# Attention followed by two MLPs: inner values of the first MLP by 768-token blocks, and y's remainders partly on GpSimd

## The chip, the cores and the metric

The kernel runs on one core of a Trainium2 chip. The metric is the device time of the whole program in microseconds (us), median of three runs. Engines are called PE (TensorE, matrix products), ACT (ScalarE), DVE (VectorE), POOL (GpSimd) and SP (SyncE, which issues DMAs). PSUM is the accumulator memory that PE writes; SBUF is the working memory.

## What is computed

```python
a  = softmax(phi, over the 576 positions)          # 4 batches, 8 heads, 32 memory slots
km, vm = a.T @ k, a.T @ v                           # 32 x 64 per head
x  = softmax(q @ km.T / 8) @ vm                     # joined over heads: 2304 tokens x 512
y  = ((x @ w_a) * (x @ w_b)) @ w_out                # first MLP,  1536 inner values
h  = y @ w_in
out = where(h > 0, h, exp(min(h, 0)) - 1) @ w_out2  # second MLP, 2048 inner values
```

The weights arrive as 64-bit floats. Each product is made from two parts per operand: a rounded part ("hi") and the remainder ("lo"), and three products hi·hi, hi·lo, lo·hi are summed in PSUM.

## The kernel before

**Stages.** An attention prologue runs over the 4 batches of 576 tokens (to about 75 us of the span). Then the first MLP (MLP1) runs, to 421 us, and the second (MLP2), to the end. The 2304 tokens are therefore 4 batches `b` of S = 576 for MLP1, and 3 blocks `t` of TB = 768 for MLP2. The result `y` of MLP1 is kept in three SBUF tiles of one block each.

**MLP1.** The inner values come in NF1 = 12 groups `f` of 128. For each `f`, `step_u` (line 483) forms the weights of the group folded with vm (two steps `u(f,0)`, `u(f,1)`), which needs the two converted units `("ab", f, 0)` and `("ab", f, 1)`. `steps_ab(f, b)` (line 576) makes two PE steps of 12 products of 288 columns each: x·w_a, copied out by ACT (line 597), and x·w_b, multiplied into that by DVE (line 599). One step later ACT rounds the product into `gh` (line 600), and two steps later DVE takes the remainder into `gl` (line 601). `gh` and `gl` are tiles of one group and one batch, nine buffers each. `run_o1(b, f)` (line 650) then multiplies all groups of batch `b` that are waiting (up to G = 3) by w_out: `steps_o1` (line 621) makes four PE steps, one for each 128 of the 512 outputs, each of 6 products of 288 columns per waiting group. The result is added to `y` from PSUM: by ACT where it is the first sum of these tokens (line 640), otherwise by DVE (line 642). A batch crosses block borders, so `y_parts` (line 606) cuts this into one, two or three instructions.

**Order.** All engines run in the order in which the program issues (the schedule is written by hand). The list at lines 667 to 674 fixes the order of the `u` and `ab` steps. A call of `run_o1` is appended to `pend` when `(f + b) % 3 == 2` (line 689) and made two `ab` calls later (three for f = 0), line 687. `step` (line 229) issues the PE work of a step, then, in the order "0f1a2", a share of the weight conversion ("f"), the step's own evacuation ("a"), and what was deferred to this step ("2", the default place).

**Weight conversion.** Each 64-bit unit is converted by seven small DVE pieces, slots 0 to 6 of `piece` (line 147), with ACT helping. `fill(amount)` issues pieces by credit: 1 per `ab` and `u` step, 3 per o1 step, 2.5 per `h` step, 3 or 6 per o2 step. `weights(key)` (line 192) issues all pieces that are still missing for a unit at the place where PE needs it. Slot 3 also issues, on POOL's queue, the DMA that loads the unit three further on (lines 98 to 106, 170). Pieces are held back when four short or four long units are alive.

**Border of the two MLPs.** After the last `ab` step the loop at line 707 runs what is left of o1: one group of b = 1, two of b = 2 and three of b = 3. In between, `split_y` (line 699) cuts a block of `y` into `yh` (ACT) and `yl` (DVE), four chunks of 128 x 768 per block, at once where it is called. Block 2 is split at line 717.

**MLP2.** `step_h(f, t)` (line 721) makes 24 products of 384 columns with `yh`/`yl` of block t, then a chain of ACT and DVE work forms the activation. For f = 0 the blocks come in the order 0, 1, 2. `steps_o2` (line 759) makes the products with w_out2, 512 columns each. PSUM serves four tiles in turn, each of which holds one step's result until it has been evacuated.

Of the kernel before, what the change touches and what calls it, by code (L numbers as in the profile page):

```python
# [7 lines left out]
F32 = mybir.dt.float32  # L8
F32R = mybir.dt.float32r
# [4 lines left out]
AF = mybir.ActivationFunctionType  # L14
ALU = mybir.AluOpType
# [6 lines left out]
def attention_then_two_mlps(ctx, tc, q, kv, kv_left, phi, w_ab, w_o1, w_i2, w_o2, out):  # L22
# [13 lines left out]
    nc = tc.nc  # L36
    B, P, KC, S = q.shape
# [4 lines left out]
    NF1, NF2 = w_ab.shape[0], w_i2.shape[0]  # L42
# [1 line left out]
    SM = NJ * P  # L44
    LEFT = S - SM
    HS = S // 2
    G = 3
    TB = 768
    NB = NT // TB
    HB = TB // 2  # L50
# [14 lines left out]
    def pone(name):  # L65
        return pstile(name)[:, 0] if len(pss) == 2 else ps1.tile([P, 512], F32, tag="one", name=name)

    def split_sb(hi, lo, src):
        nc.scalar.activation(out=hi, in_=src, func=AF.Copy)  # L69
        nc.vector.tensor_tensor(out=lo, in0=src, in1=hi.bitcast(F32), op=ALU.subtract)  # L70


    NRAW, NSHORT, NLONG = 3, 4, 4
# [140 lines left out]
    RATE_AB, RATE_U, RATE_O1 = 1.0, 1.0, 3.0  # L214
    RATE_H, RATE_O2 = 2.5, 3.0
# [5 lines left out]
    def defer(steps, fn, at=2):  # L221

        later.append([steps, fn, at])
# [257 lines left out]
    u_t, g_t = {}, {}  # L481
# [28 lines left out]
    with tc.manual_schedule():  # L510
# [65 lines left out]
        def steps_ab(f, b, amount):  # L576
            u = u_t.pop((f, b))
            a_sb = pb.tile([P, 2, HS], F32, tag="a_sb", name="a_sb", bufs=3)
            flat = a_sb.rearrange("p a s -> p (a s)")
            gh = pb.tile([P, S], F32R, tag="gh", name="gh", bufs=9)  # L580
            gl = pb.tile([P, S], F32R, tag="gl", name="gl", bufs=9)
            g_t[f, b] = gh, gl
            for n in range(2):
                ps = pstile("ab_ps")

                def pe():
                    for kk in range(2):
                        for i, (w, x) in enumerate(((0, xhi), (0, xlo), (1, xhi))):
                            for h in range(2):
                                nc.tensor.matmul(  # L590
                                    ps[:, h, 0:HS], u[:, kk, w, n * P:n * P + P], x[b][:, kk, h * HS:(h + 1) * HS],
                                    start=(kk == 0 and i == 0), stop=(kk == 1 and i == 2),
                                )

                def evac():
                    if n == 0:
                        nc.scalar.activation(out=a_sb, in_=ps[:, :, 0:HS], func=AF.Copy)  # L597
                    else:
                        nc.vector.tensor_tensor(out=a_sb, in0=a_sb, in1=ps[:, :, 0:HS], op=ALU.mult)  # L599
                        defer(1, lambda: nc.scalar.activation(out=gh, in_=flat, func=AF.Copy))  # L600
                        defer(2, lambda: nc.vector.tensor_tensor(
                            out=gl, in0=flat, in1=gh.bitcast(F32), op=ALU.subtract))

                step(pe, evac, amount)

        def y_parts(c, t0, ps):


            if t0 // TB == (t0 + S - 1) // TB:
                o = t0 % TB  # L610
                yield ps[:, :, 0:HS], yv[t0 // TB][:, c, o:o + S].rearrange("p (h s) -> p h s", h=2)
                return
            for h in range(2):
                done = 0
                while done < HS:
                    blk, o = divmod(t0 + h * HS + done, TB)
                    w = min(HS - done, TB - o)
                    yield ps[:, h, done:done + w], yv[blk][:, c, o:o + w]
                    done += w

        def steps_o1(b, fs, amount):
            for c in range(KC):
                ps = pstile("o1_ps")

                def pe():
                    cc = slice(c * P, (c + 1) * P)
                    for n, f in enumerate(fs):
                        wh, wl = weights(("o1", f))
                        gh, gl = g_t[f, b]
                        for i, (w, g) in enumerate(((wh, gh), (wh, gl), (wl, gh))):  # L630
                            for h in range(2):
                                nc.tensor.matmul(  # L632
                                    ps[:, h, 0:HS], w[:, cc], g[:, h * HS:(h + 1) * HS],
                                    start=(n == 0 and i == 0), stop=(n == len(fs) - 1 and i == 2),
                                )

                def evac():
                    for src, dst in y_parts(c, b * S, ps):
                        if fs[0] == 0:
                            nc.scalar.activation(out=dst, in_=src, func=AF.Copy)  # L640
                        else:
                            nc.vector.tensor_tensor(out=dst, in0=src, in1=dst, op=ALU.add)

                step(pe, evac, amount)
            for f in fs:
                g_t.pop((f, b))

        used1 = {}

        def run_o1(b, f):  # L650
            fs = [x for x in range(NF1) if (x, b) in g_t and x <= f]
            steps_o1(b, fs, RATE_O1)
            for x in fs:
                used1[x] = used1.get(x, 0) + 1
                if used1[x] == B:
                    drop(("o1", x))

        last = B - 1
# [18 lines left out]
        for kind, *args in order:  # L677
            if kind == "do":
                args[0]()
            elif kind == "u":  # L680
                step_u(*args, RATE_U)
            else:
                f, b = args
                steps_ab(f, b, RATE_AB)
                for e in pend:
                    e[0] -= 1
                if pend and pend[0][0] <= 0:
                    run_o1(*pend.pop(0)[1:])
                if (f + b) % G == G - 1:
                    pend.append([2 if f else 3, b, f])  # L690
        es_u.close()
        es_a.close()

# [2 lines left out]
        pc = es_2.enter_context(tc.tile_pool(name="pc", bufs=2, reuse_waits="tile"))  # L696
        ysp = {}

        def split_y(blk, pool):
            hi = pool.tile([P, KC, TB], F32R, tag=f"yh{blk}", name=f"yh{blk}", bufs=1)  # L700
            lo = pool.tile([P, KC, TB], F32R, tag=f"yl{blk}", name=f"yl{blk}", bufs=1)
            for c in range(KC):
                split_sb(hi[:, c], lo[:, c], yv[blk][:, c])
            ysp[blk] = hi, lo

        flush_later()
        for b in range(B):
            if any((x, b) in g_t for x in range(NF1)):
                run_o1(b, NF1 - 1)
            if b == 1:  # L710
                split_y(0, pc)
            if b == 2:
                split_y(1, pc)
        es_b.close()
        es_0.close()
        pd = es_2.enter_context(tc.tile_pool(name="pd", bufs=2, side="right", reuse_waits="tile"))
# [4 lines left out]
        def step_h(f, t):  # L721
            ps = pstile("h_ps")
            yh, yl = ysp[t]
            wh, wl = [x.rearrange("p (c f) -> p c f", c=KC) for x in weights(("i2", f))]
            gh = pd.tile([P, TB], F32R, tag="g2h", name="g2h", bufs=6)
            gl = pd.tile([P, TB], F32R, tag="g2l", name="g2l", bufs=6)
            g2[f, t] = gh, gl

            def pe():
                for c in range(KC):  # L730
                    for i, (w, x) in enumerate(((wh, yh), (wh, yl), (wl, yh))):
                        for h in range(2):
                            nc.tensor.matmul(  # L733
                                ps[:, h, 0:HB], w[:, c], x[:, c, h * HB:(h + 1) * HB],
                                start=(c == 0 and i == 0), stop=(c == KC - 1 and i == 2),
                            )

            e = pc.tile([P, 2, HB], F32, tag="e", name="e", bufs=2)
            flat = e.rearrange("p a s -> p (a s)")
            th = pc.tile([P, 2, HB], F32, tag="th", name="th", bufs=1)  # L740


            def negative():
                nc.scalar.activation(out=e, in_=ps[:, :, 0:HB], func=AF.Relu, scale=-1.0)  # L744

            def functions():
                nc.scalar.activation(out=th, in_=e, func=AF.Tanh, scale=-0.5)
                nc.scalar.activation(out=e, in_=e, func=AF.Exp, scale=-1.0)  # L748

            def both_signs():  # L750
                nc.vector.scalar_tensor_tensor(out=e, in0=e, scalar=1.0, in1=th, op0=ALU.add, op1=ALU.mult)  # L751
                nc.vector.tensor_tensor(out=e, in0=e, in1=ps[:, :, 0:HB], op=ALU.max)
                defer(1, lambda: nc.scalar.activation(out=gh, in_=flat, func=AF.Copy), 0)
                defer(1, lambda: nc.vector.tensor_tensor(
                    out=gl, in0=flat, in1=gh.bitcast(F32), op=ALU.subtract), 1)

            step(pe, [negative, functions, both_signs], RATE_H, ORDER_H)

        def steps_o2(t, fs, last):

# [115 lines left out]
```

## Time and profile before

| | us |
|---|---|
| median of 3 runs (828.2 to 829.19) | 829.03 |
| the profiled execution's own time | 829.17 |
| its span, first to last instruction | 827.4 |
| PE busy | 790.7 |
| DVE busy | 593.1 |
| ACT busy | 396.5 |
| POOL busy | 40.5 |

The rows further down come from the profiled execution. In the groups of instructions the last column is the time for which the engine stood idle just ahead of these instructions, and what released it. In the chain of waits a row tells which work the end of the program hung on at that moment. Ends of matrix products are modelled, so rates are read from the spacing of long runs of them.

### The profile page before, as it was taken

What the parts mean: (1) busy time and instruction counts of PE and PEld (TensorE: products, weight loads), DVE (VectorE), ACT (ScalarE), POOL (GpSimd) and SP (SyncE); (2) the same over time, 40 slices, a digit from 0 to 9 for tenths busy, and PEclk for the clock granted to TensorE, in tenths of its full rate; (3) what the DMA queues carried; (4) which work ended last, traced back from release to release, by engine and by line L of the source; (5) the groups of instructions that cost most, each with busy time, mean ns of one, the idle gap of its engine ahead of it and who ended that gap; (6) DMA issues with size and microseconds to landing.
All of it is one profiled execution on the core that took longest, in us unless ns stands there. A gap on an engine that the chain in (4) does not pass through costs nothing.

```text
span 827.4 us, 14253 instructions
## 1 busy us (share of the span) xinstructions
PE 790.7 (96%) x6032; PEld 729.4 (88%) x6032; DVE 593.1 (72%) x979; ACT 396.5 (48%) x608; POOL 40.5 (5%) x87
## 2 busy tenths in 40 slices
PE   4588899999999999999999999999999999999997
PEld 3477789999999999999999899888999889998896
DVE  3488988678877886667778842787777786776464
ACT  2434576554434433343357754556654556553350
POOL 2000000000000000000000000000000000000000
PEclk9599999999999999999999999999999999999999
DMA  9882022112220221001000200111111110100006
GB/s 325 293 289 102 1 83 97 58 71 78 77 77 27 78 77 51 27 27 51 26 27 26 77 26 15 62 50 35 45 52 51 51 51 26 51 0 1 1 1 229
DMA packets 16815, 57.79 MB, mean 70 GB/s; under 512 B 1776, under 2 KB 1776, under 8 KB 16752
## 3 DMA queue, kind: packets, MB, share of 16 engines
q0 software_dynamic: 9360, 34.08, 11.7%
q1 hardware_dynamic: 7392, 22.81, 7.8%
q8 instruction: 47, 0.77, 0.4%
q14 instruction: 16, 0.13, 0.0%
HBM read 52.17 MB, written 4.72 MB: 69 GB/s over the span
## 4 chain that ended last, share of the span: by engine, by line
PE 91%; DVE 4%; ACT 2%; DMA 2%; issue 0%; SPq 0%; ACTq 0%; DVEq 0%
PE o_ps L776 24%; PE h_ps L733 24%; PE o_ps L632 18%; PE ab_ps L590 18%; PE u_ps L497 2%; PE sc L426 2%; DMA raw<-in_w_ab_dram 1%; PE pk L386 1%; DVE ssm L460 1%; DVE y L465 1%; PE tp_x L473 0%; PE tp_a L362 0%; DVE y L453 0%; DVE smx L452 0%; DMA phi_t<-in_phi_dram 0%
## 5 line engine op out<-in xcount | busy, mean ns | idle before, releaser
L590 PE MATMUL ab_ps<-xhi,u 128*128 128x288 f32 x768 | 139.4, 298 | 3.7 <-ACT xhi L69 2.9
L590 PEld LDWEIGHTS ab_ps<-xhi,u 128*128 128x128 f32 x768 | 114.1, 189 | 9.0 <-issue 3.2
L776 PE MATMUL o_ps<-ulh,g2h 128*128 128x512 f32 x288 | 113.7, 395 | 0.0
L776 PE MATMUL o_ps<-ull,g2h 128*128 128x512 f32 x288 | 113.6, 394 | 0.0
L776 PE MATMUL o_ps<-ulh,g2l 128*128 128x512 f32 x288 | 103.0, 395 | 0.0
L751 DVE SCALAR_TENSOR_TENSOR e<-e,th 128x768 f32<-128x768 f32 x48 | 46.0, 958 | 75.0 <-ACT e L748 74.6
L733 PE MATMUL h_ps<-yh,usl 128*128 128x384 f32 x384 | 97.8, 335 | 0.0
L733 PE MATMUL h_ps<-yl,ush 128*128 128x384 f32 x384 | 97.7, 335 | 0.0
L733 PE MATMUL h_ps<-yh,ush 128*128 128x384 f32 x384 | 97.7, 335 | 0.0
L744 ACT ACTIVATE e<-h_ps 128x768 f32<-128x768 f32 x48 | 39.0, 813 | 95.8 <-PE h_ps L733 93.6
L632 PE MATMUL o_ps<-gh,ulh 128*128 128x288 f32 x384 | 82.5, 296 | 0.6 <-DVE u L507 0.4
L632 PE MATMUL o_ps<-gl,ulh 128*128 128x288 f32 x384 | 82.2, 296 | 0.0
L632 PE MATMUL o_ps<-gh,ull 128*128 128x288 f32 x384 | 82.2, 296 | 0.0
L590 PE MATMUL ab_ps<-xlo,u 128*128 128x288 f32 x384 | 82.1, 295 | 0.0
L597 ACT ACTIVATE a_sb<-ab_ps 128x576 f32<-128x576 f32 x48 | 31.3, 652 | 86.4 <-PE ab_ps L590 86.4
L733 PEld LDWEIGHTS h_ps<-yh,ush 128*128 128x128 f32 x384 | 69.5, 188 | 1.3
L599 DVE TENSOR_TENSOR a_sb<-a_sb,ab_ps 128x576 f32<-128x576 f32 x48 | 36.1, 752 | 46.5 <-PE ab_ps L590 44.8
L733 PEld LDWEIGHTS h_ps<-yh,usl 128*128 128x128 f32 x384 | 69.4, 188 | 0.0
L733 PEld LDWEIGHTS h_ps<-yl,ush 128*128 128x128 f32 x384 | 69.3, 188 | 0.0
L776 PEld LDWEIGHTS o_ps<-ulh,g2l 128*128 128x128 f32 x288 | 54.0, 187 | 13.2
L776 PEld LDWEIGHTS o_ps<-ulh,g2h 128*128 128x128 f32 x288 | 54.0, 187 | 12.6
L776 PEld LDWEIGHTS o_ps<-ull,g2h 128*128 128x128 f32 x288 | 54.0, 187 | 12.5
(93 smaller groups left out, 1338.4 us busy)
## 6 DMA issues: line engine op xcount, KB each, us to landing
raw<-in_w_o_dram POOLq DMA_DIRECT2D x27, 512.0 KB, 3.5
raw<-in_w_ab_dram POOLq DMA_DIRECT2D x22, 512.0 KB, 3.6
kv_t<-in_kv_dram SPq DMA_DIRECT2D x16, 512.0 KB, 10.1
raw<-in_w_i_dram POOLq DMA_DIRECT2D x16, 512.0 KB, 3.6
y<-in_q_dram SPq DMA_DIRECT2D x8, 576.0 KB, 8.8
out_dram<-y SPq DMA_DIRECT2D x8, 512.0 KB, 2.9
phi_t<-in_phi_dram SPq DMA_DIRECT2D x3, 576.0 KB, 11.8
left_t<-in_kv_left_dram SPq DMA_DIRECT2D x4, 256.0 KB, 12.1
```

What stands on the lines that cost most here:

```text
L386: nc.tensor.matmul(pk[M * h:M * h + M, D * u:D * u + D], a[0:P if j < NJ else LEFT, u, j, M * h:M * h + M], rows, start=(j == 0), stop=(j ...
L426: nc.tensor.matmul(sc[:, u, j * P:(j + 1) * P], qs[u][:, t, j * P:(j + 1) * P], kt[:, u, t * P:(t + 1) * P], start=(t == 0), stop=(t == 1))
L460: nc.vector.tensor_reduce(out=sm, in_=at, op=ALU.add, axis=AX.X)
L497: nc.tensor.matmul(ps[j:j + M, o, k * 256:k * 256 + 256], vt[r, 2 * k + c, 2 * p + o], w[r, c * 256:c * 256 + 256], start=True, stop=True, ...
L590: nc.tensor.matmul(ps[:, h, 0:HS], u[:, kk, w, n * P:n * P + P], x[b][:, kk, h * HS:(h + 1) * HS], start=(kk == 0 and i == 0), stop=(kk == ...
L597: nc.scalar.activation(out=a_sb, in_=ps[:, :, 0:HS], func=AF.Copy)
L599: nc.vector.tensor_tensor(out=a_sb, in0=a_sb, in1=ps[:, :, 0:HS], op=ALU.mult)
L632: nc.tensor.matmul(ps[:, h, 0:HS], w[:, cc], g[:, h * HS:(h + 1) * HS], start=(n == 0 and i == 0), stop=(n == len(fs) - 1 and i == 2),)
L733: nc.tensor.matmul(ps[:, h, 0:HB], w[:, c], x[:, c, h * HB:(h + 1) * HB], start=(c == 0 and i == 0), stop=(c == KC - 1 and i == 2),)
L744: nc.scalar.activation(out=e, in_=ps[:, :, 0:HB], func=AF.Relu, scale=-1.0)
L751: nc.vector.scalar_tensor_tensor(out=e, in0=e, scalar=1.0, in1=th, op0=ALU.add, op1=ALU.mult)
L776: nc.tensor.matmul(ps[:, k, :], g[:, c * P:(c + 1) * P], w, start=(f == fs[0] and i == 0), stop=(f == fs[-1] and i == 2),)
```

## The change

- `gh` and `gl` become tiles of one group and one 768-token block, seven buffers each. A batch writes one or two parts: batch 0 lies in block 0; batch 1 puts 192 tokens in block 0 and 384 in block 1; batch 2 puts 384 in block 1 and 192 in block 2; batch 3 lies in block 2. ACT and DVE round and subtract part by part.
- o1 runs per block: six products of 384 columns per group and step; the sum with `y` is one instruction of 768 columns; `y_parts` is gone.
- `run_o1(t, f)` is appended when batch `b = t + 1` of a group with `(f + t) % 3 == 2` was issued, and made one `ab` call later (two for f = 0).
- At the border the o1 steps convert weights at 0.5 instead of 3.0 pieces a step, and the `h` steps of f = 0 at 0.5 instead of 2.5.
- The splits of blocks 0 and 1 are deferred, chunk c by c + 1 steps, and their `yl` goes to GpSimd; block 2 stays on DVE, at once.

```diff
-    G = 3
+    G, NG = 3, 7
-    def split_sb(hi, lo, src):
+    def split_sb(hi, lo, src, eng=nc.vector):
         nc.scalar.activation(out=hi, in_=src, func=AF.Copy)
-        nc.vector.tensor_tensor(out=lo, in0=src, in1=hi.bitcast(F32), op=ALU.subtract)
+        eng.tensor_tensor(out=lo, in0=src, in1=hi.bitcast(F32), op=ALU.subtract)
...
-            gh = pb.tile([P, S], F32R, tag="gh", name="gh", bufs=9)
-            gl = pb.tile([P, S], F32R, tag="gl", name="gl", bufs=9)
-            g_t[f, b] = gh, gl
+            parts, done = [], 0
+            while done < S:
+                t, o = divmod(b * S + done, TB)
+                if o == 0:
+                    g_t[f, t] = [pb.tile([P, TB], F32R, tag=x, name=x, bufs=NG) for x in ("gh", "gl")]
+                w = min(S - done, TB - o)
+                parts.append((flat[:, done:done + w], *[x[:, o:o + w] for x in g_t[f, t]]))
+                done += w
...
-                        defer(1, lambda: nc.scalar.activation(out=gh, in_=flat, func=AF.Copy))
-                        defer(2, lambda: nc.vector.tensor_tensor(
-                            out=gl, in0=flat, in1=gh.bitcast(F32), op=ALU.subtract))
+                        defer(1, lambda: [nc.scalar.activation(out=gh, in_=a, func=AF.Copy) for a, gh, _ in parts])
+                        defer(2, lambda: [nc.vector.tensor_tensor(out=gl, in0=a, in1=gh.bitcast(F32), op=ALU.subtract)
+                                          for a, gh, gl in parts])
...
-                                    ps[:, h, 0:HS], w[:, cc], g[:, h * HS:(h + 1) * HS],
+                                    ps[:, h, 0:HB], w[:, cc], g[:, h * HB:(h + 1) * HB],
...
-                    for src, dst in y_parts(c, b * S, ps):
-                        if fs[0] == 0:
-                            nc.scalar.activation(out=dst, in_=src, func=AF.Copy)
-                        else:
-                            nc.vector.tensor_tensor(out=dst, in0=src, in1=dst, op=ALU.add)
+                    src, dst = ps[:, :, 0:HB], yv[t][:, c].rearrange("p (h s) -> p h s", h=2)
+                    if fs[0] == 0:
+                        nc.scalar.activation(out=dst, in_=src, func=AF.Copy)
+                    else:
+                        nc.vector.tensor_tensor(out=dst, in0=src, in1=dst, op=ALU.add)
...
-                if (f + b) % G == G - 1:
-                    pend.append([2 if f else 3, b, f])
+                t = b - 1
+                if b and (f + t) % G == G - 1:
+                    pend.append([1 if f else 2, t, f])
...
-                split_sb(hi[:, c], lo[:, c], yv[blk][:, c])
+                (defer if blk + 1 < NB else now)(c + 1, lambda c=c: split_sb(hi[:, c], lo[:, c], yv[blk][:, c],
+                                                              nc.gpsimd if blk + 1 < NB else nc.vector))
...
-        for b in range(B):
-            if any((x, b) in g_t for x in range(NF1)):
-                run_o1(b, NF1 - 1)
-            if b == 1:
-                split_y(0, pc)
-            if b == 2:
-                split_y(1, pc)
+        for t in range(NB):
+            if any((x, t) in g_t for x in range(NF1)):
+                run_o1(t, NF1 - 1, 0.5)
+            if t + 1 < NB:
+                split_y(t, pc)
...
-            step(pe, [negative, functions, both_signs], RATE_H, ORDER_H)
+            step(pe, [negative, functions, both_signs], RATE_H if f else 0.5, ORDER_H)
```

## Rows read from the trace of the kernel before

**Rows 1.** The page: busy time by engine, and slices of the span.

```profile
PE 790.7 (96%) x6032; PEld 729.4 (88%) x6032; DVE 593.1 (72%) x979; ACT 396.5 (48%) x608; POOL 40.5 (5%) x87
PE   4588899999999999999999999999999999999997
...
PEclk9599999999999999999999999999999999999999
```

**Rows 2.** Chain of waits in order of time: start us, us, what.

```profile
141.72 9.60 PE o_ps L632 x72
...
411.42 9.82 PE o_ps L632 x72
421.24 25.01 PE h_ps L733 x144
...
463.00 12.60 PE o_ps L776 x54
475.60 12.50 PE h_ps L733 x72
```

**Rows 3.** PE's waits over the span: us in total, times, longest.

```profile
PE ab_ps L590 <- ACT xhi L69: 2.9, 1, 2.9
...
PE ab_ps L590 <- ACT y L640: 0.8, 1, 0.8
PE o_ps L632 <- DVE u L507: 0.4, 1, 0.4
```

**Rows 4.** Timeline around the first o1 steps: start us, us, instruction, idle before.

```profile
113.28 0.42 PE L632 MATMUL o_ps<-gh,ulh 128*128 128x288 f32 x2
...
113.55 0.75 DVE L599 TENSOR_TENSOR a_sb<-a_sb,ab_ps 128x576 f32<-128x576 f32 x1 [1.37 <-PE ab_ps L590]
...
114.22 0.75 DVE L601 TENSOR_TENSOR gl<-a_sb,gh 128x576 fp32r<-128x576 f32 x1
...
114.89 0.42 DVE L178 TENSOR_TENSOR lw<-lw,p 128x512 bf16<-128x512 bf16 x1
...
115.34 0.69 DVE L185 TENSOR_TENSOR ush<-a,lw 128x512 f32<-128x512 f32 x1
...
116.57 0.66 PE L497 MATMUL u_ps<-ush,vt 64*32 64x256 f32 x16
```

**Rows 5.** Groups by line: count, busy us, mean ns, idle before.

```profile
L754 DVE TENSOR_TENSOR g2l<-e,g2h 128x768 fp32r<-128x768 f32 x48 | 45.8, 954 | 9.6 <-ACT g2h L753 9.5
L642 DVE TENSOR_TENSOR y<-o_ps,y 128x288 f32<-128x288 f32 (+3 forms) x120 | 45.7, 429 | 19.2 <-PE o_ps L632 19.0
L753 ACT ACTIVATE g2h<-e 128x768 fp32r<-128x768 f32 x48 | 40.5, 844 | 35.4 <-DVE e L752 35.4
L601 DVE TENSOR_TENSOR gl<-a_sb,gh 128x576 fp32r<-128x576 f32 x48 | 36.1, 751 | 4.6 <-ACT gh L600 4.5
L600 ACT ACTIVATE gh<-a_sb 128x576 fp32r<-128x576 f32 x48 | 32.7, 680 | 10.0 <-DVE a_sb L599 9.8
```

**Rows 6.** Timeline of DVE just behind an o1 start at 388.49 us.

```profile
388.76 0.76 DVE L599 TENSOR_TENSOR a_sb<-a_sb,ab_ps 128x576 f32<-128x576 f32 x1 [0.72 <-PE ab_ps L590]
389.43 0.75 DVE L601 TENSOR_TENSOR gl<-a_sb,gh 128x576 fp32r<-128x576 f32 x1
390.10 0.42 DVE L160 TENSOR_SCALAR a<-a 128x512 f32<-128x512 f32 x1
```

**Rows 7.** Groups of POOL by form: count, busy us, mean ns.

```profile
L103 POOL DMA_DIRECT2D raw<-in_w_o_dram x27 | 14.5, 537 | 307.1 <-DVE p L173 131.4 <-ACT g2h L753 114.4 <-DVE a L168 20.0
L522 POOL COPY pair<-ident 128x32 f32<-128x32 f32 x8 | 1.4, 211 | 0.0
L520 POOL COPY y<-ident 128x64 f32<-128x64 f32 x4 | 0.9, 237 | 0.1
```

**Rows 8.** Timeline of DVE at the border of the two MLPs.

```profile
406.92 3.55 DVE L70 TENSOR_TENSOR yl<-y,yh 128x768 fp32r<-128x768 f32 x4
...
413.57 3.56 DVE L70 TENSOR_TENSOR yl<-y,yh 128x768 fp32r<-128x768 f32 x4
```

More of the change, by code (lines that the diff above doesn't have):

```diff
@@ L599, in evac, with steps_o1 @@
                         nc.vector.tensor_tensor(out=a_sb, in0=a_sb, in1=ps[:, :, 0:HS], op=ALU.mult)
-                        defer(1, lambda: nc.scalar.activation(out=gh, in_=flat, func=AF.Copy))
-                        defer(2, lambda: nc.vector.tensor_tensor(
-                            out=gl, in0=flat, in1=gh.bitcast(F32), op=ALU.subtract))
+                        defer(1, lambda: [nc.scalar.activation(out=gh, in_=a, func=AF.Copy) for a, gh, _ in parts])
+                        defer(2, lambda: [nc.vector.tensor_tensor(out=gl, in0=a, in1=gh.bitcast(F32), op=ALU.subtract)
+                                          for a, gh, gl in parts])
                 step(pe, evac, amount)
[L606 to L621, printed above, removed]
+        def steps_o1(t, fs, amount):
             for c in range(KC):
@@ L628, in pe @@
                         wh, wl = weights(("o1", f))
-                        gh, gl = g_t[f, b]
+                        gh, gl = g_t[f, t]
                         for i, (w, g) in enumerate(((wh, gh), (wh, gl), (wl, gh))):
@@ L637, in evac, with run_o1 @@
                 def evac():
-                    for src, dst in y_parts(c, b * S, ps):
-                        if fs[0] == 0:
-                            nc.scalar.activation(out=dst, in_=src, func=AF.Copy)
-                        else:
-                            nc.vector.tensor_tensor(out=dst, in0=src, in1=dst, op=ALU.add)
+                    src, dst = ps[:, :, 0:HB], yv[t][:, c].rearrange("p (h s) -> p h s", h=2)
[3 more added lines that the diff above has]
+                        nc.vector.tensor_tensor(out=dst, in0=src, in1=dst, op=ALU.add)
                 step(pe, evac, amount)
             for f in fs:
-                g_t.pop((f, b))
+                g_t.pop((f, t))
         used1 = {}
-        def run_o1(b, f):
-            fs = [x for x in range(NF1) if (x, b) in g_t and x <= f]
-            steps_o1(b, fs, RATE_O1)
+        def run_o1(t, f, amount=RATE_O1):
+            fs = [x for x in range(NF1) if (x, t) in g_t and x <= f]
+            steps_o1(t, fs, amount)
             for x in fs:
                 used1[x] = used1.get(x, 0) + 1
-                if used1[x] == B:
+                if used1[x] == NB:
                     drop(("o1", x))
@@ L697, in attention_then_two_mlps, with now @@
         ysp = {}
+        def now(_, fn):
+            fn()
         def split_y(blk, pool):
```

## Prediction, made before the changed kernel was run

> **What bounds the kernel now.** I read the page's busy times and slices first: PE is busy for 790.7 of 827.4 us, and from the sixth slice on every slice but the last has the digit 9 [rows 1]. DVE, the next, has 593.1. So whatever the change saves on DVE or ACT is worth nothing by itself; it must shorten PE's own work or a wait of PE. The chain of waits confirms it: between 130 us and the end it is made of PE pieces that follow each other without gaps, and the border of the MLPs, at 421 us, is one of those joints [rows 2]. The view of PE's waits leaves little to win behind the prologue: one wait of 0.8 us and one of 0.4 us, both near 121 to 123 us, and the 2.9 us on ACT at 93 us, where the attention of the last batches still runs beside MLP1 [rows 3].
>
> So the questions are: what does PE pay for the new shape of product, and does a new wait open?
>
> **The products (the gain).** Before, o1 has 12 groups x 4 batches x 4 steps x 6 = 1152 products of 288 columns. After, 12 x 3 x 4 x 6 = 864 of 384. The columns are the same 331,776. A run of 72 products of 288 takes 9.60 us, 133.3 ns each; 72 of 384 in the `h` steps, same operand types and 128x128 stationary tile, take 12.50 us, 173.6 ns, and 144 take 25.01 us, 173.7 ns [rows 2]. So 1152 x 0.1333 = 153.6 us becomes 864 x 0.1737 = 150.1 us: 3.5 us less, all on the path. Put otherwise: at 2.4 GHz, the level granted there [rows 1], the columns take 120 and 160 ns, so some 13.5 ns stick to every product whatever its width, and 288 products fewer save 288 x 0.0133 - 864 x 0.0004 = 3.5 us.
>
> The Trainium skill (TensorE: Matmul & The Clock Gate, "Back-to-back issue gap") gives a warm gap of columns divided by 2.4 GHz plus about 2.5 ns. By that 288 products fewer would save only 0.7 us; our two rows carry five times that overhead, so I go by the rows, and keep the rule as a rival.
>
> **A wait that the new order opens (a loss).** I followed the credit rule through the list of steps. Before, the first o1 call (batch 2, group 0) lies ahead of `u(2,0)`, and its four steps issue 12 pieces, two of which finish the unit ("ab", 2, 1) that `u(2,0)` needs. After, that call waits for batch 3 and falls behind `u(2,0)` and `u(2,1)`. At `u(2,0)` two pieces (slots 5 and 6) are missing, and `weights` issues them on the spot, behind DVE's product and remainder of the step before. The trace shows just this queue: product at 113.55, remainder at 114.22, slot 5 at 114.89, slot 6 from 115.34 to 116.03, while PE does its o1 products from 113.28 and comes to `u` at 116.57 [rows 4]. Without these, PE starts `u(2,0)` at 113.28, does its first half in about half a microsecond (an estimate: 16 instructions of the 0.66 us row, which overlaps its successor) and stands until 116.1: 2.3 us lost. Bounds: 0 (if the pieces run earlier) and 3.0 (one more DVE instruction of 0.75 us ahead of them).
>
> Against that, the two waits of 0.8 and 0.4 us came from the same burst of 12 pieces in 3.2 us of PE, with one ACT queue behind [rows 3]. Replayed with the new order, the bursts meet steps of 1.04 and 2.08 us instead of 0.8 and 1.6, and PSUM tiles come free 0.7 us ahead of PE or better. I take them as gone, with 1.2 us as the other end. Net at this place: 2.3 - 1.2 = 1.1 us lost (0 to 2.3).
>
> **More, smaller instructions.** Batches 1 and 2 round and subtract in two parts: 24 more on ACT, 24 more on DVE. From 576 and 768 columns, ACT goes 680 to 844 ns, so 0.19 us is fixed; DVE 751 to 954, so 0.14 us [rows 5]: 4.6 and 3.4 us, on engines with room. Only in the prologue is ACT on the path, once, ahead of the 2.9 us wait [rows 3]: 0.2 us. The sums with `y` become 44 DVE instructions of about 0.95 us, 42 us where there were 45.7 in 120 [rows 5]; off the path, nothing.
>
> **Less slack for o1.** A call now comes one `ab` call after its last batch, not two. Its last group's `gl` is then issued behind the newest product on DVE. At an o1 start of 388.49 us DVE takes that product at 388.76 and a remainder at 389.43, done at 390.18, 1.7 us after PE began [rows 6]. PE needs it only after two groups of 6 products and two more: 14 x 0.174 = 2.4 us. 0.7 us is left, so I charge nothing; if DVE is behind by one more instruction of 0.75 us, PE waits under 0.3 us in each of some 10 calls, 3 us in all. Weights: counted to the end, no other unit is missing when PE asks; the lead is 8 pieces or more in the later `u` steps and o1 calls (it was 13 or more), and from `h(1,1)` on the count is the same as before. At most 7 inner tiles are alive, as many as there are.
>
> **The border.** The left-over o1 shrinks from six groups of 576 tokens to three of 768; that moves products, it removes none. From the end T of the last `ab` step PE has 72 x 0.174 = 12.5 us of o1, then the `h` steps of 4.17 us each. POOL gets eight remainders of 128x768 and one DMA issue. No row shows its subtraction. A copy takes 211 ns for 32 columns and 237 for 64 [rows 7]: 185 ns and 0.81 ns a column, so 0.81 us for one input over 768; a second read pass gives 1.43, a write pass on top 2.06. I take 1.75 us, between the last two, as reads and writes may share a path. The first can start when ACT has made the last `gh` and the first `yh`: 0.3 + 0.75 + 0.68 + 0.85 = 2.6 us after T. End of the eighth: 2.6 + 0.54 + 8 x 1.75 = 17.1 us. The last chunk of block 1 is wanted at 12.5 + 4.17 + 3 x 1.04 + 0.35 = 20.1 us. It is hidden, with 3 us. At 2.06 us each it ends at 19.6, still hidden; if DVE's four remainders of 0.95 us for block 2 had to take turns with it there, 3.8 us later, and PE would wait 3.3. DVE is freed of 2 x 3.55 us [rows 8], but it wasn't the bound. Block 2 on DVE has 8.3 us from the end of o1 for 3.6 us of work, as before.
>
> The Trainium skill (SBUF — State Buffer, "Who interferes with whom") says that a DVE instruction with two SBUF inputs and a GpSimd one that reads SBUF lock each other out for a whole instruction. By that the four `yl` of block 2 could hold up the last two or three GpSimd ones, 0.95 us each: the end would move to about 20 us, just in time. It speaks against the change. No row here shows both engines so engaged.
>
> **Sum.** The span is 827.4; -3.5 + 1.1 + 0.2 gives 825.2. The profiled execution took 829.17 for that span, 1.77 more: 827.0. It lies 0.14 above the median, so as a difference to the median that is -2.0 us, 0.25%. I predict 827.0.
>
> **Rivals.** (1) GpSimd too slow, ending slower. Place: block 1 in `h(0,1)`. With the strict turns costed from DVE's four remainders (4 x 0.95 = 3.8 us) PE is late by 3.1 + 8p + 3.8 - 20.1. The gain of 2.0 and the 0.2% beyond it are used up from p = 2.1 us. For: POOL's row of two-input work is missing. Against: the copy's slope. At p = 2.5, 6.8 us late: 833.8. (2) The shorter slack bites: 3 us over the calls, 830.0. For: DVE is busy for 72% of the span [rows 1]. Against: rows 6. (3) The new wait at `u(2,0)` doesn't show, the old ones go: 827.0 - 2.3 = 824.7. Against: the queue in rows 4. (4) The change doesn't do what it says: 384-column products in o1 gain only the 0.7 us of the page's rule, or nothing: 829.8 to 830.5. Against: the `h` row.
>
> **How the numbers follow.** Forecast (826 to 828.3): 0.54; rival 1: 0.14; rival 2: 0.17; rival 3: 0.10; rival 4: 0.05. A measurement of this kernel tells some 0.2% (1.66 us) from no change, so "faster" is below 827.4. It takes 0.40 of the forecast and rival 3: 0.50. "Same" takes the forecast's other 0.14, most of rival 2 and rival 4: 0.34. "Slower", above 830.7, is rival 1 and a rest of rival 2: 0.16. Range 824.5 to 831.5: it leaves out most of rival 1 and the edge of rival 3.
>
> **What would show it.** Right: runs of 72 o1 products of 12.5 us; a PE wait of about 2.3 us ahead of the second half of `u(2,0)` near 114 us; no PE wait on POOL near the border; POOL's subtraction below 2.1 us. Wrong: 384-column o1 at 178 ns, many short waits of o1 on DVE `gl`, or a wait of `h` on POOL.

## The result, and the profile after

The changed kernel takes 835.09 us (median of 5 runs, 831.26 to 837.77) where the kernel before takes 829.03 (5 runs beside it, 828.2 to 830.13): a ratio of 1.0067 [1.0042, 1.0091], 0.67% slower. The forecast was 827.0 and its range ended at 831.5, so the time came out 8 us above the forecast and 3.6 us above the range, slower where faster was forecast. The profiled execution took 835.95 us with a span of 834.2.

The page of the changed kernel, busy times and slices:

```profile
PE 789.7 (95%) x5744; PEld 727.9 (87%) x5744; DVE 597.7 (72%) x919; ACT 397.1 (48%) x612; POOL 54.5 (7%) x95
...
PE   4589899999999999999969999999999999999998
...
POOL 2000001000000000000340000000000000000000
PEclk9599999999999999999989999999999999999999
```

POOL's row of the kernel before, which [rows 1] leaves out:

```profile
POOL 2000000000000000000000000000000000000000
```

Against before one thing is new: around the border of the MLPs, in the slices from 396 to 438 us, POOL has a 3 and a 4, and in the second of them (417 to 438 us) PE, which had a 9 there, has a 6, with an 8 in the granted clock. No other digit of PE's row moved by more than one, so the loss must lie at the border. PE's waits say the same (us in total, times, longest):

```profile
PE o_ps L622 <- DVE y L632: 7.3, 1, 7.3
...
PE u_ps L497 <- DVE ush L185: 2.1, 1, 2.1
```

The 0.8 and 0.4 us of [rows 3] are gone, 2.1 us at `u(2,0)` are there, as forecast, and there is a single wait of 7.3 us that the forecast didn't have: o1 waits for a sum of `y` on DVE, that is for a PSUM tile that this sum has yet to free. The chain of waits in order of time (start us, us, what), first at an undisturbed o1 call and then at the border:

```profile
147.40 12.48 PE o_ps L622 x72
...
411.94 1.73 DVE y L632 x2
413.68 10.23 DVE p L173
423.90 0.88 DVE y L632
424.82 3.69 PE o_ps L622 x12
428.51 25.02 PE h_ps L726 x144
```

The chain leaves PE, passes through one DVE instruction of 10.23 us (line 173, the mask of a weight conversion) and comes back. Of before, the same place was a run of PE pieces without a gap [rows 2]. The timeline there, POOL and DVE together (start us, us, engine line instruction, idle before):

```profile
409.53 1.87 POOL L70 TENSOR_TENSOR yl<-y,yh 128x768 fp32r<-128x768 f32 x1 [12.29 <-ACT yh L69]
410.29 1.66 DVE L168 SCALAR_TENSOR_TENSOR a<-raw,a 128x512 uint32<-128x512 uint32 x1
411.87 1.81 DVE L632 TENSOR_TENSOR y<-o_ps,y 128x768 f32<-128x768 f32 x2
412.24 0.57 POOL L103 DMA_DIRECT2D raw<-in_w_o_dram  x1 [0.84 <-DVE a L168]
412.84 10.78 POOL L70 TENSOR_TENSOR yl<-y,yh 128x768 fp32r<-128x768 f32 x6
413.60 10.30 DVE L173 TENSOR_SCALAR p<-a 128x512 uint16<-128x512 uint16 x1
423.82 1.81 DVE L632 TENSOR_TENSOR y<-o_ps,y 128x768 f32<-128x768 f32 x2
424.82 1.01 PE L622 MATMUL o_ps<-gh,ulh 128*128 128x384 f32 x2 [7.28 <-DVE y L632]
425.72 1.96 POOL L70 TENSOR_TENSOR yl<-y,yh 128x768 fp32r<-128x768 f32 x1 [2.11 <-ACT yh L69]
```

Read it from the top. The first remainder runs on POOL. On DVE slot 3 of a conversion (line 168) follows; it issues the load of a later weight unit, and that load stands in POOL's queue behind the first remainder. Then POOL has six remainders in a row, 412.84 to 423.62. DVE starts the mask, slot 4, at 413.60, and the mask ends at 423.90, when POOL has run dry. POOL runs dry because its eighth remainder needs a `yh` that ACT makes from a sum standing behind the mask. Behind the mask on DVE stand the sums with `y`; without these no PSUM tile of o1 comes free; so PE stands. The same stretch by windows (us, busy time of PE, PEld, DVE, ACT, POOL, then the granted clock, the DMA share and GB/s):

```profile
407.15:417.50 10.35, 10.35 (x60) 10.07 (x59) 9.51 (x7) 6.95 (x10) 7.10 (x5) 1.00 0.16 51
417.50:424.82 7.32, 0.04 (x1) 0.00 (x0) 7.32 (x3) 0.02 (x1) 6.12 (x4) 0.73 0.00 0
424.82:428.51 3.69, 3.69 (x13) 3.69 (x14) 3.48 (x5) 3.29 (x4) 1.96 (x1) 0.61 0.00 0
428.51:453.53 25.02, 25.02 (x146) 25.02 (x145) 18.47 (x23) 17.09 (x23) 0.57 (x1) 1.00 0.07 22
```

So the border costs 428.51 - 407.15 = 21.4 us where 72 x 0.1737 = 12.5 us are products: 8.9 us more, of which 7.3 are PE's wait and 1.6 are the last 12 products at a granted clock of 0.61 on the mean, between the levels 1.2 and 2.4 GHz (3.69 us where 12 x 0.1737 = 2.08). Take these off, and the span is 834.2 - 8.9 = 825.3; the forecast's span was 825.2. That these agree to 0.1 us is partly luck: by the two chains of waits the attention prologue took 0.7 us longer in this execution and MLP2 0.5 us less, and neither was forecast so. Between them, from the `ab` products that start at 106.83 us before and at 107.53 after to the first `h` step, the change saves 2.3 us without the 8.9, where 3.5 - 1.1 = 2.4 was forecast.

### The profile page after: what moved, and what is told of

Its sections match the earlier page's. It is cut to its first block, busy times and chain, and to the rows that moved or that the text cites. A ratio compares the mean times of both kernels' runs of the same rounds, so it can differ in the third digit from the quotient of the medians.

```text
span 834.2 us, 13589 instructions
## 1 busy us (share of the span) xinstructions
PE 789.7 (95%) x5744; PEld 727.9 (87%) x5744; DVE 597.7 (72%) x919; ACT 397.1 (48%) x612; POOL 54.5 (7%) x95
## 4 chain that ended last, share of the span: by engine, by line
PE 88%; DVE 6%; DMA 3%; ACT 2%; SPq 0%; issue 0%; DVEq 0%; ACTq 0%
PE o_ps L769 24%; PE h_ps L726 24%; PE ab_ps L595 18%; PE o_ps L622 17%; PE u_ps L497 2%; DMA phi_t<-in_phi_dram 2%; PE sc L426 1%; DVE p L173 1%; DMA y<-in_q_dram 1%; DVE ssm L460 1%; PE pk L386 1%; DVE y L465 1%; DVE y L453 0%; DVE smx L452 0%; ACT y L454 0%; DVE y L632 0%
## 5 line engine op out<-in xcount | busy, mean ns | idle before, releaser
L595 PEld LDWEIGHTS ab_ps<-xhi,u 128*128 128x128 f32 x768 | 116.2, 191 | 8.3 <-issue 4.0
L622 PE MATMUL o_ps<-gh,ulh 128*128 128x384 f32 x288 | 74.0, 337 | 7.3 <-DVE y L632 7.3
L622 PE MATMUL o_ps<-gl,ulh 128*128 128x384 f32 x288 | 73.5, 336 | 0.0
L622 PE MATMUL o_ps<-gh,ull 128*128 128x384 f32 x288 | 73.4, 335 | 0.0
```

What stands on the lines that cost most here:

```text
L595: nc.tensor.matmul(ps[:, h, 0:HS], u[:, kk, w, n * P:n * P + P], x[b][:, kk, h * HS:(h + 1) * HS], start=(kk == 0 and i == 0), stop=(kk == ...
L622: nc.tensor.matmul(ps[:, h, 0:HB], w[:, cc], g[:, h * HB:(h + 1) * HB], start=(n == 0 and i == 0), stop=(n == len(fs) - 1 and i == 2),)
```

## The experiments

Each kernel is the changed kernel with a small edit, or the kernel before with a stream of instructions added at its end to measure a cost by itself. Medians stand with the ratio to the kernel before and its 95% interval. The theories: A, DVE's mask, which reads and writes SBUF only, is locked out while POOL has remainders to do, because of its form; B, every DVE instruction at the border, the sums too, is slowed by POOL; C, the remainders take so long that the products of o1 no longer cover them, whatever DVE converts; D (which came later), it is the load issued on POOL between the remainders that makes the lock last; G (with D), it is the position: an instruction gets in at the first two boundaries between remainders and is held to the end of the run at any later one; H (last), it is the place within a long run of remainders that nothing has interrupted.

**First the changed kernel once more**, with no edit.

> The changed kernel once more, on the same chip as its variants. A: a second profile shows slot 4's mask held for several GpSimd remainders; 829 to 836. D: the mask is held only behind the DMA. If the first measurement was a matter of the chip, 825 to 828.

835.81 us, 1.0065 [1.0041, 1.0089]. The mask takes 10.31 us from 413.77, PE waits 7.3. The hold is a property of the kernel and not an accident of one execution.

**No conversion at the border.**

```
-                run_o1(t, NF1 - 1, 0.5)
+                run_o1(t, NF1 - 1, 0.0)
```

> The changed kernel with no weight-conversion piece issued during the eight o1 steps of the border (rate 0 instead of 0.5); the four pieces move into the h steps behind it. Three theories of the 8.9 us that the border lasts longer than its 12.5 us of products. A, lock: one single-input DVE instruction (slot 4, 0.42 us before, 10.3 us in the changed run) is shut out while GpSimd's remainders follow each other without a pause, and PE waits for the sum with y queued behind it. Expects no PE wait at the border, full clock there, and a time of about 826 to 827.5. B, turns: every DVE instruction with an SBUF operand is slowed beside GpSimd, the sums with y too. Expects each sum at 1.5 us or more and about 830. C, cover: the border has too few products left to hide the splits, whatever GpSimd does. Expects 833 to 836, as the changed kernel.

825.41 us, 0.9965 [0.9948, 0.9981]. Chain of waits and POOL's timeline of this kernel:

```profile
404.44 12.49 PE o_ps L622 x72
416.93 23.09 PE h_ps L726 x133
```
```profile
406.85 14.63 POOL L70 TENSOR_TENSOR yl<-y,yh 128x768 fp32r<-128x768 f32 x8 [12.29 <-DVE gl L606]
```

POOL still does all eight remainders, 1.83 us each, and PE goes from o1 to `h` without a gap. That leaves neither C (the cover is long enough) nor B (the sums take 0.95 us beside POOL). It is the conversion that meets the remainders.

**No GpSimd at the border**: the remainders of all blocks on DVE.

```
-  nc.gpsimd if blk + 1 < NB else nc.vector
+  nc.vector
```

> The changed kernel with all of y's remainders on DVE, everything else as it is (same deferred places, same pieces). A: no instruction is held; DVE has some 16 us of work (8 x 0.95 remainders, 8 x 0.95 sums) for 12.5 us of products, so the border costs 1 to 4 us of PE waits: 827.5 to 831. B: as A. C: as the changed kernel or worse, 833 to 838.

827.05 us, 0.9973 [0.9958, 0.9988]; PE doesn't wait at the border, and once for 0.4 us in the `h` steps at 452 us. That is just better than the 827.5 to 831 that A and B expected. So the products and the blocks of 768 alone are worth what was forecast for the whole change. The interval overlaps with the run without conversion: remainders on POOL gain nothing that can be measured here, and where they meet the conversion as in the changed kernel they cost 8 us (835.09 against 827.05).

**Which instruction is held?** The rates of the last `ab` step and of the border shift which slots of the conversion fall among the remainders: the slots 5 and 6, with two inputs, or the mask alone.

```
-                steps_ab(f, b, RATE_AB)
+                steps_ab(f, b, RATE_AB if (f, b) != (NF1 - 1, last) else 2.0)   # mask alone: 1.5
...
-                run_o1(t, NF1 - 1, 0.5)
+                run_o1(t, NF1 - 1, 0.25)
```

> The changed kernel with the pieces shifted by two: the last ab step issues two more (rate 2), the border at rate 0.25 issues only slot 5 (a product of two 16-bit tiles, both in SBUF) at its fourth step and slot 6 (a sum of two SBUF tiles) at its eighth. A: two-input instructions wait for one remainder at most (the one in the changed run took 1.66 us where it takes 0.68), so slot 5 ends within 2.3 us and the time is 826 to 828. B: some 829 to 831. C: 833 to 836.

> Twin of the kernel with the shifted pieces: shifted by one only (rate 1.5 in the last ab step), so that at the fourth step of the border stands slot 4, the single-input 16-bit mask, and slot 5 at the eighth. A: slot 4 is held until GpSimd pauses, 5 to 11 us, and the time is 830 to 837, unlike its twin. B: as its twin, 829 to 831. C: 833 to 836.

825.56 us, 0.995 [0.9933, 0.9967], and 826.86 us, 0.9976 [0.996, 0.9992]. Slot 5 of the first and the mask of the second:

```profile
410.01 1.49 DVE L178 TENSOR_TENSOR lw<-lw,p 128x512 bf16<-128x512 bf16 x1
```
```profile
411.13 1.50 DVE L173 TENSOR_SCALAR p<-a 128x512 uint16<-128x512 uint16 x1
```

Both take 1.5 us where they need some 0.4: they wait for the remainder that runs, and then get in. The mask too. So A, which expected 830 to 837 of the second, falls as I had put it: the form alone doesn't starve. PE waits at the border in neither; the second has one PE wait of 1.3 us on DVE at 453 us, in MLP2.

**The same, later among the remainders**: border rate 0.2 in place of 0.25, the slots one step of o1 later.

> The changed kernel with its border pieces shifted so that slot 4's mask stands at the fifth of the eight steps (rate 1.5 in the last ab step, 0.2 in the border), in the middle of GpSimd's remainders, and GpSimd issues no DMA there. A: the mask is held until the last remainder, some 8 to 11 us; the four sums behind it come late, PE waits 3 to 7 us ahead of the h steps: 829 to 834. B and D: the mask ends within 2.3 us and the time is 825 to 826.5.

> Twin of the kernel with the mask in the middle: at the same place stands slot 5, a product of two 16-bit SBUF tiles (rate 2 in the last ab step). A, B and D: it waits for one or two remainders, ends within 4 us, no PE wait at the border, 824.5 to 826.5. If a two-input instruction is shut out like the mask, 829 to 834.

825.87 us, 0.9957 [0.9944, 0.9971], and 824.7 us, 0.9947 [0.993, 0.9963]. The mask of the first, with POOL beside it:

```profile
406.82 0.53 POOL L103 DMA_DIRECT2D raw<-in_w_o_dram  x1 [9.77 <-ACT a_sb L602]
...
409.34 16.31 POOL L70 TENSOR_TENSOR yl<-y,yh 128x768 fp32r<-128x768 f32 x8 [1.99 <-ACT yh L69]
...
412.69 0.65 DVE L173 TENSOR_SCALAR p<-a 128x512 uint16<-128x512 uint16 x1
```

The mask is asked for in the second remainder, as in the changed kernel, and waits 0.2 us, so A falls here again. What differs: here the load was issued 2.5 us ahead of the remainders, there it lies between the first and the second. That is theory D.

**The cost by itself.** Behind the kernel before, streams of five POOL subtractions of 128x768, and in each a DVE instruction that becomes ready some 0.85 us after the stream begins; no load.

```
+ for i in range(5):
+     nc.gpsimd.tensor_tensor(out=o, in0=one, in1=gate, op=ALU.subtract)
+ nc.vector.tensor_scalar(...)     # then others, one form in each stream
```

> The kernel before with a measurement added behind its end: seven times, GpSimd runs five subtractions of 128x768 (two SBUF inputs) without a pause between them, and one DVE instruction becomes ready about 0.9 us after the first of them has started. The seven forms: slot 4's 16-bit mask, slot 1's 32-bit shifts, slot 0's maximum and minimum (all with a single SBUF input), slot 5's product of 16-bit tiles, slot 3's two-input instruction, a remainder of 768 columns (all with two SBUF inputs), a sum of PSUM and SBUF of 768 columns. Its time as a whole says nothing. A, lock: the three single-input forms, 0.42 us alone, last until the five subtractions are over, 7 to 9 us; the three two-input forms wait for one or two subtractions, 1.5 to 4.5 us; the sum with PSUM takes its 0.95 us. B, turns: every form with an SBUF input takes 1 to 3 us. D, the DMA that GpSimd had just issued in the changed run is what held the mask: here is none, so the single-input forms last at most 2.3 us.

In order: POOL's stream around the max/min, the max/min itself, a remainder, a sum from PSUM:

```profile
826.45 9.02 POOL L840 TENSOR_TENSOR pool_out<-one_x,gate 128x768 f32<-128x768 f32 x5 [0.95 <-ACT gate L836]
...
827.28 1.26 DVE L851 TENSOR_SCALAR dve_out<-dve_in 128x512 f32<-128x512 f32 x1 [1.17 <-ACT dve_in L837]
...
857.48 1.79 DVE L860 TENSOR_TENSOR dve_out<-one_x,dve_in 128x768 f32<-128x768 f32 x1 [8.72 <-ACT dve_in L837]
...
871.03 0.96 DVE L865 TENSOR_TENSOR dve_out<-px_ps,one_x 128x768 f32<-128x768 f32 x1 [11.77 <-PE px_ps L864]
```

826.45 + 9.02/5 = 828.25 is the end of the first subtraction, and the max/min ends 0.29 us behind that: it stood until the running subtraction was over, as every other form did that has its operands in SBUF only (the mask and the shift fell on DVE's own end work and told nothing). The sum from PSUM took its usual 0.96. None was held longer than one subtraction.

The Trainium skill (SBUF — State Buffer, "Who interferes with whom") gives this as a lock that whoever issues first holds for the whole instruction; 1.25 to 1.79 us in this probe agree with that. The 10.3 us of the changed kernel, six instructions long, don't.

**The load moved off POOL.** Only the one load that slot 3 issues at the border goes to SP's queue.

```
-            load_unit()
+            load_unit(nc.sync if n == index['i2', 2] else nc.gpsimd)
```

> The changed kernel with one difference: the weight load that slot 3 issues at the border goes out on SP's queue instead of GpSimd's. The lock theory in its first form has fallen: without a DMA among the remainders a single-input instruction got in at the next one's end (0.65 to 1.50 us), yet the changed kernel held the mask for 10.3 us twice. D, the DMA issue of GpSimd, 0.57 us between its first and second remainder, is what makes the difference. Expects the mask done within 2.3 us, no PE wait at the border and 824.5 to 827. G, position: a single-input instruction gets in only at the first two boundaries of a run of remainders, where GpSimd still waits for its inputs; later it is held to the end of the run. Expects the mask, which now meets the third remainder, held for 6 us or more and 829 to 836.

825.31 us, 0.9969 [0.9955, 0.9983]; PE doesn't wait at the border, and once for 0.3 us in the `h` steps at 451 us. POOL and the mask:

```profile
407.55 17.45 POOL L70 TENSOR_TENSOR yl<-y,yh 128x768 fp32r<-128x768 f32 x8 [12.29 <-DVE gl L606]
...
411.62 0.41 DVE L173 TENSOR_SCALAR p<-a 128x512 uint16<-128x512 uint16 x1
```

Same slots in the same order as in the changed kernel, and the mask takes 0.41 us. The whole loss is gone, as D expected; G, with a hold of 6 us or more, falls.

**The load moved in.** The reverse: the kernel with the mask one step later (825.87 us) with its load put between the first and the second remainder.

```
-            load_unit()
+            if n != index['i2', 2]:
+                load_unit()
...
-  lambda c=c: split_sb(...)
+  lambda c=c: [load_unit() if (blk, c) == (0, 1) else None, split_sb(...)]
```

> The kernel with the mask in the middle of the border, with one difference: the load that GpSimd had issued ahead of its remainders is issued between the first and the second of them, as in the changed kernel. D: the mask, 0.65 us without that, is held until the remainders are over, 8 us or more; PE waits ahead of the h steps: 828 to 834. G: the mask comes in at a boundary of the same number as before and lasts 2.3 us at most: 824.5 to 827.

834.65 us, 1.0075 [1.0059, 1.0092]. POOL, then the mask:

```profile
409.16 0.58 POOL L103 DMA_DIRECT2D raw<-in_w_o_dram  x1
409.76 12.60 POOL L70 TENSOR_TENSOR yl<-y,yh 128x768 fp32r<-128x768 f32 x7
...
410.69 11.95 DVE L174 TENSOR_SCALAR p<-a 128x512 uint16<-128x512 uint16 x1
```

The mask is held for all seven remainders behind the load, PE waits 6.2 us, and 8.8 us are lost against the twin (9.8 by the two ratios); D had expected 828 to 834. With the two edits together the place of one load makes the loss and unmakes it.

**The cost by itself, with the load.** Streams as above, the DVE instruction ready some 3.5 us in; every second stream has a load of 512 KB between its first and second subtraction.

> The kernel before with six cases behind its end: GpSimd runs five subtractions of 128x768; one DVE instruction becomes ready about 3.5 us after the first has started, so in the second (or third) of them; in every second case GpSimd issues a 512 KB load between the first and the second subtraction. Forms: mask without and with load, maximum and minimum without and with, product of 16-bit tiles without and with. Its time as a whole says nothing. D: without load 0.4 to 2.3 us each; with load the mask and the maximum last until the fifth subtraction is over, 5 us or more. G: mask and maximum last 4 us or more with load and without; the product 2.3 us at most in both.

A max/min without and with the load, then a product of 16-bit tiles without and with it:

```profile
828.58 0.43 DVE L852 TENSOR_SCALAR dve_out<-dve_in 128x512 f32<-128x512 f32 x1 [3.79 <-ACT dve_in L838]
...
836.88 0.57 POOL L844 DMA_DIRECT2D dma<-in_w_o_dram  x1
837.48 7.08 POOL L841 TENSOR_TENSOR pool_out<-one_x,gate 128x768 f32<-128x768 f32 x4
838.58 6.26 DVE L852 TENSOR_SCALAR dve_out<-dve_in 128x512 f32<-128x512 f32 x1 [9.58 <-ACT dve_in L838]
...
848.96 0.43 DVE L856 TENSOR_TENSOR dve_out<-dve_in 128x512 bf16<-128x512 bf16 x1 [4.12 <-ACT dve_in L838]
...
858.97 6.26 DVE L856 TENSOR_TENSOR dve_out<-dve_in 128x512 bf16<-128x512 bf16 x1 [9.58 <-ACT dve_in L838]
```

With the load, both forms end 0.3 us behind POOL's last subtraction (837.48 + 7.08 = 844.56; 838.58 + 6.26 = 844.84); without it they take 0.43. One input or two makes no difference. The mask's pair fell on DVE's end work again.

The two cases without a load came ready only 0.2 us ahead of the end of a subtraction, those with one 0.7 us ahead; so the moment has to be ruled out too. Other rows do it. Without a load, instructions that came ready 1.0 us (the max/min of the first probe) and 1.2 us (slot 5 and the mask at rate 0.25) ahead of the end of a subtraction got in at that end; with a load, those 0.7 us (here), 0.9 us (the load moved in) and 1.1 us (the changed kernel) ahead of it did not.

**Can the hold come without a load?** The mask two steps of o1 later still, no load among the remainders (1.5 in the last `ab` step, 0.145 at the border).

> The kernel with the mask in the middle of the border, with the mask two steps later (rate 0.145), so that it meets the fourth or fifth remainder; no DMA among them. D: within 2.3 us. G: held until the eighth remainder is over, 5 us or more. The time hardly moves in either case, since only two sums stand behind it: 824 to 829.

826.82 us in one run, and the mask was held after all:

```profile
407.68 14.68 POOL L70 TENSOR_TENSOR yl<-y,yh 128x768 fp32r<-128x768 f32 x8 [1.98 <-ACT yh L69]
...
414.52 8.12 DVE L173 TENSOR_SCALAR p<-a 128x512 uint16<-128x512 uint16 x1
```

8.12 us from the fourth remainder to the end of the eighth: D's limit of 2.3 us falls here, and G had this one right. PE waits once, 1.4 us at 452 us in MLP2; the kernel with the mask at rate 0.25 has the same wait (1.3 us) without a hold, so the hold cost little, as only two sums stood behind it. So the load is not the only way in. Three more rows are of this kind: the first remainder that DVE does itself, late in POOL's run, took 4.45, 4.66 and 4.63 us (in the run without conversion, in the one with slots 5 and 6 one step later, and in the last run below), each time until POOL was done, and cost PE nothing. In the other four kernels without a load among POOL's remainders (the two with rate 0.25, the one with the mask one step later, the one with the load on SP), the same DVE remainders took turns with POOL's, 2.6 us at most, and POOL's run stretched to 16.3 us or more. Theory H put this down to the place: the later in an uninterrupted run, the longer the hold. Two kernels at hand speak against it: with the mask and with slot 5 one step later, that slot gets in behind POOL's second remainder in both, and the first remainder of DVE begins 11.00 us after POOL's run did in both (409.34 and 406.86). In the first it gets in at once, in the second it is held:

```profile
420.34 1.02 DVE L70 TENSOR_TENSOR yl<-y,yh 128x768 fp32r<-128x768 f32 x1
```
```profile
417.86 4.66 DVE L70 TENSOR_TENSOR yl<-y,yh 128x768 fp32r<-128x768 f32 x1
```

H was tried by itself behind the kernel before, with eight subtractions in a row and a max/min ready in the second, third, fourth or fifth.

> The kernel before with five cases behind its end: GpSimd runs eight subtractions of 128x768 with nothing between them, and one DVE instruction (maximum and minimum, one SBUF input, 0.42 us alone) becomes ready about 3.4, 5.1, 6.8 or 8.5 us after the first has started, that is in subtraction 2, 3, 4 or 5; in the fifth case one such instruction comes at 3.4 and another at 8.5 us. Its time as a whole says nothing. D, only the load matters: at most 2.3 us in every case. H, a run of subtractions that nothing has interrupted shuts DVE out from about the fourth on, and a load among them does so at once: the cases in subtraction 2 and 3 at most 2.3 us, those in 4 and 5 until the eighth is over, 8 and 6 us; in the fifth case the early one gets in and opens the way, so the late one takes 2.3 us at most. If only the count from the start matters, the late one of the fifth case is held for 6 us too.

```profile
851.57 14.32 POOL L838 TENSOR_TENSOR pool_out<-one_x,gate 128x768 f32<-128x768 f32 x8 [0.95 <-ACT gate L835]
858.52 0.44 DVE L845 TENSOR_SCALAR dve_out<-dve_in 128x512 f32<-128x512 f32 x1 [16.59 <-ACT dve_in L844]
...
875.55 0.46 DVE L845 TENSOR_SCALAR dve_out<-dve_in 128x512 f32<-128x512 f32 x1 [16.59 <-ACT dve_in L844]
```

No hold at any of the places, the fourth and fifth (shown) included: 0.43 to 0.46 us each, and 0.43 and 0.80 us for the two of the fifth case. By itself it isn't a clean refusal of H, as each max/min came ready only 0.1 to 0.5 us ahead of the end of a subtraction. What makes the four holds without a load stays open.

**A version that is better than both.** The conversion is moved out of the border, and forward in the `ab` steps ahead of `u(2,0)` as well, so that no piece is missing there.

```
-                steps_ab(f, b, RATE_AB)
+                steps_ab(f, b, RATE_AB if (f, b) not in ((0, last), (NF1 - 1, last)) else 2.0)
...
-                run_o1(t, NF1 - 1, 0.5)
+                run_o1(t, NF1 - 1, 0.2)
```

> The kernel with the two-input piece in the middle of the border, and besides the two pieces that PE waits for at u(2,0) are issued earlier (rate 2 instead of 1 in the two steps of batch 3, group 0), on top of DVE's idle time there. If the 2.1 us that PE stands at u(2,0) are a wait for these pieces and nothing else, the wait goes and the time is 822 to 823.5, some 6 us under the kernel before. If something else is late there, 824.5 to 826.

823.71 us (821.84 to 824.37), 0.9929 [0.9912, 0.9945], just above the 822 to 823.5 that were expected if nothing else was late at `u(2,0)`. Chain of waits near `u(2,0)` and at the border:

```profile
108.42 6.58 PE ab_ps L595 x48
115.01 1.89 PE u_ps L497 x64
...
404.15 12.50 PE o_ps L622 x72
```

No DVE piece stands between the `ab` products and `u(2,0)` any more, and the border is 72 products without a gap. How much of it the wait at `u(2,0)` is worth isn't told: the same kernel with that wait had 0.9947 [0.993, 0.9963], and the intervals overlap.

## Why the prediction was wrong, point by point

**The products: right.** 72 in 12.48 us, forecast 12.5. Rival 4, by which the change would gain 0.7 us or nothing from them, is out.

**The wait at `u(2,0)`: right**, 2.1 us for 2.3, with the queue that was read from [rows 4]: `gl`, slot 5, slot 6, then PE. The waits of 0.8 and 0.4 us went, as forecast.

**The shorter slack (rival 2): didn't come.** No wait of o1 on `gl` is in the list of PE's waits.

**POOL's subtraction: right in size**, 1.79 to 1.96 us (median 1.85) for 1.75; its row was missing, and a value picked between two bounds from copies came out, in part by luck.

**The border: wrong, and all of the miss.** Two things failed in this step. First, I costed the load on POOL at its 0.54 us and the lock between the engines at one turn of 0.95 us, for DVE's four own remainders alone; the pieces of conversion that the border's rate of 0.5, a part of the diff, puts into the same stretch weren't weighed against the remainders at all. Second, I asked when POOL would be done and who needs its result (block 1 at 20.1 us), and not who would wait for DVE if POOL held DVE up: the sums with `y`, the PSUM tiles, PE. The chain runs through DVE; POOL's results were in time. The term stood at 0 and measured 8.9 us: 7.3 of wait, 1.6 of products at a lower granted clock.

**Rival 1 had the border, the sign and about the size (833.8), by another mechanism; that the size fits is luck.** It needed a subtraction of 2.1 us or more and a wait of `h` on POOL; the subtraction took 1.85, and the wait is of o1 on DVE. Its chance of 0.14 was for slow arithmetic; a hold of DVE was not among the cases, so 0.16 for slower was too little for an overlap for which no row existed.

What is shown: the load's place makes the hold and the loss (there with it in 835.09, 835.81 and 834.65 us; gone without it in 825.31 and 825.87). With a load among back-to-back subtractions DVE was shut out to their end five times of five. What is only argued is why. The Trainium skill (GPSIMD Engine Reference, "Instruction dispatch") says that a core of GpSimd begins the next instruction without waiting for the other cores. If issuing the load put some of these cores behind the others, there might be no moment between two subtractions in which none of them is at work, and DVE would get in only when the queue is empty. No run here looks at the cores one by one, and the four holds without a load would need another cause of such an offset.

## What to carry to other kernels

When work is moved to GpSimd beside a busy DVE, ask less how long GpSimd takes than what DVE has to do in that stretch with operands in SBUF only, and what is queued behind that: one held instruction of 0.4 us kept every sum behind it, and so PE. Keep GpSimd-issued loads out of a run of back-to-back GpSimd arithmetic (issue them ahead, or from another queue), or keep DVE's SBUF-only work out of it; each of these alone took some 9 us of loss away here, though the one hold of the mask without a load shows that the first is no guarantee. An overlap of two engines for which the trace has no row is a term to be bounded from above by the whole run of the other engine, not by one of its instructions.

## What the runs showed that I had not expected

- A DVE instruction of 0.41 to 0.43 us was held for 10.3, 10.3, 11.95, 6.26 and 6.26 us, to the end of the POOL subtractions behind a POOL load; one-input and two-input forms alike. Sums with one operand in PSUM were not held (0.94 to 0.96 us).
- Without a load the wait mostly ended with the running subtraction (1.25 to 1.79 us in all in the first probe), but four times late in a run it went on to its end (8.12, 4.45, 4.66 and 4.63 us), once at a place and moment at which another kernel's instruction got in at once.
- A subtraction of 128x768 with two inputs takes 1.79 to 1.96 us on POOL and 0.95 on DVE.
- After 7.3 us without products PE's granted clock was 0.61 over the next 3.7 us, and 1.00 from 428.5 us on: the wait cost 1.6 us more than its own length.
